# A whole order of steps written anew, with the softmax guards off VectorE and space between steps of VectorE and GpSimd, in an attention and gating kernel

## The chip, the cores and the metric

One core of one Trainium2 chip runs the kernel. The metric is the device time of one execution in microseconds (us). The engines are PE (TensorE matmul; its weight loads are shown apart as PEld), DVE (VectorE), ACT (ScalarE), POOL (GpSimd) and SP (SyncE, which here only issues DMAs). Each works through its own queue in order and waits where an operand or a buffer is not ready.

## What is computed

For each of 8 batches and 8 heads, 512 tokens `x` (64 wide) and 32 states read each other by softmax attention. The joined result, 576 rows of 512 channels, goes through a causal convolution of five taps per channel, a sigmoid gate, a product with `x @ w_val`, and a product with `w_out`.

```python
scores = scale * np.matmul(x, state.transpose(0, 1, 3, 2))
a = np.exp(scores - scores.max(-1, keepdims=True))
a /= a.sum(-1, keepdims=True) + 1e-09
xread = np.matmul(a, state)
...                                   # scores2, a2: the same with x and state exchanged
sread = np.matmul(a2, x)
x = np.concatenate([xread, sread], axis=2)   # then as (8, 576, 512)
gate = 1.0 / (1.0 + np.exp(-gate_pre))       # gate_pre: five taps of conv_w along the sequence
return (gate * (x @ w_val) @ w_out).astype(np.float32)
```

## The kernel before

The work is cut into 882 small steps, 858 of which run. Most of a step is one instruction on ACT, DVE or POOL, or one group of matmuls. A hand-written table of numbers, `ORDER`, gives the one order in which all steps are recorded; every engine's queue is that order with the other engines' steps left out. A letter behind a number picks the engine where the step can run on several: `a` ACT, `v` DVE, `g` POOL. A second table, `PLACES`, gives each tile its buffer: eight PSUM banks `ps0` to `ps7`, and named slots in SBUF. A tile that takes over a slot waits for the last reader of the tile before it. So the two tables set the queues and all the waits; the functions only say what a step does.

For each batch b the steps are: load `xT` and `x`; `scores` (PE, tile `sc`); `scores_T` (DVE transposes it into `sl`), `max_n`, `sub_n`, `exp_n`, `sum_n`, `guard_n` (adds 1e-9 to the sums), `inverse_n`, `scale_n` and `probs` (transposes the probabilities back), which is the softmax over the states; `max_s`, `exp_s`, `sum_s` (the guard of the other softmax, 128x2 numbers), `inverse_s`, and `exp_T`, `state_read`, `state_read_copy`, `state_read_T`, `state_read_out`, which is the states' read. `state_val` (tile `sgv`) multiplies state and `w_val`. `read` (tile `xr`) gives the token's read, from which `gate_first`, `gate_last`, `gate_tap` and `gate_add` make the convolution and `gate` its tanh. `values` (tile `val`) gives the values, `gated` the product, `high` and `low` split it in two parts `gh` and `gl`, `project` (tile `op`) multiplies by `w_out`, and `store` writes 128 rows out. Batch 0 differs: its taps are multiplied into the states beforehand (`tap_state`, tile `z`), and `read_conv` then does read and convolution in 80 matmul records. The weights come as 64-bit words and are made into floats by `words_fold` (ACT), `words_clamp`, `words_low` and `words_join` (DVE). `tail` treats the 256 rows of the states at the end. Eight `warm_up` steps run ahead of the first scores and eight more between the head's matmuls.

The helper functions hold the lines that the profile names: L256, L258 and L260 are `copy` on ACT, DVE and POOL, L264 and L266 `scale`, L269 `combine`, L421, L423 and L425 `guard` on ACT, DVE and POOL. Other lines: L340 warm-up, L386 `scores`, L356 `conv_spread`, L404 `exp_T`, L414 `state_read`, L369 `state_val`, L439 `state_read_T`, L436 `state_read_copy`, L497 `read`, L512 `read_conv`, L537 `gate_tap`, L549 `gate`, L560 `values`, L563 `gated`, L568 to L570 `project`, L449 `scores_T`, L460 `max_n`, L394 `max_s`, L470 `sum_n`, L477 `inverse_n`, L486 and L488 `probs`, L320 and L325 `words_clamp` and `words_join`. This is what uses the tables:

```python
t = PLACE.get(name, tag)                       # in get(): which slot a tile stands in
...
    with tc.manual_schedule(engines=None):
        for step in ORDER:
            engine = ENGINES.get(step[-1])
            fn, args = steps[int(step.rstrip("avg"))]
            fn(*([engine] if engine else []), *args)
...
def guard(e, out, in_):                        # the three forms of a guard
        nc.scalar.activation(out, in_, AF.Identity, bias=ones[:, 1:2])
        nc.vector.tensor_scalar_add(out, in_, EPS)
        nc.gpsimd.tensor_scalar(out, in_, EPS, None, op0=ALU.add)
```

Of the kernel before, what the change touches and what calls it, by code (L numbers as in the profile page):

```python
# [833 lines left out]
```

## Time and profile before

| | |
|---|---|
| time, median of 3 runs | 214.91 us (214.18 to 215.24) |
| the profiled execution | 215.14 us, its span from first to last instruction 213.4 us |
| PE busy | 206.0 us, 97% of the span |
| DVE busy | 175.6 us, 82% |
| POOL busy | 147.8 us, 69% |
| ACT busy | 145.1 us, 68% |
| first matmul of `read_conv` | 19.00 us |
| last matmul | 210.03 us |

Times inside the span count from its first instruction. Busy shares are averages: a busy PE says that matmuls follow each other without idle time, and the waits show where they don't. A row of the timeline gives start, duration, engine, line, instruction, the tile written and the tiles read; in brackets stand the idle time ahead of it and what ended that.

### The profile page before, as it was taken

The page shows a single profiled execution, that of the slowest core. Times are in us where ns is not written, and L with a number is a line of the kernel's source. Part 1 is how long each engine was busy: PE and PEld are TensorE (multiplying, and loading weights), DVE is VectorE, ACT ScalarE, POOL GpSimd, SP SyncE. Part 2 cuts the span into 40 slices and gives each one's busy share as a digit, 9 for nine tenths or more (in the row PEclk, how much of TensorE's full clock was granted, in tenths as well). Part 3 has the DMA queues.
Part 4 walks back from the last instruction along what each step waited for, and adds up shares of the span by engine and source line. Part 5 has one row for each costly group of instructions (what it writes and reads, how often), then busy time and mean ns, then how long its engine had stood idle before and what let it go on. Part 6 is the DMA issues. An engine that isn't in the chain of part 4 may idle for free.

```text
span 213.4 us, 4629 instructions
## 1 busy us (share of the span) xinstructions
PE 206.0 (97%) x1791; PEld 150.2 (70%) x1791; DVE 175.6 (82%) x272; ACT 145.1 (68%) x306; POOL 147.8 (69%) x126
## 2 busy tenths in 40 slices
PE   8977999999999999999999999999999999999994
PEld 8754343876588677877686758688867768898883
DVE  1599898999989898999889999979997997697300
ACT  2298999985995879879947983684666473652511
POOL 1179899879989996879987899784869903620200
PEclk9999999999999999999999999999999999999999
DMA  6989990000346885510009960209400400040326
GB/s 169 397 339 335 410 413 17 0 0 3 107 193 246 292 288 151 206 54 0 3 2 321 382 281 5 98 0 290 155 0 3 151 3 0 0 149 3 146 51 197
DMA packets 9364, 31.25 MB, mean 146 GB/s; under 512 B 1130, under 2 KB 1406, under 8 KB 7422
## 3 DMA queue, kind: packets, MB, share of 16 engines
q1 hardware_dynamic: 9342, 30.96, 40.2%
q8 instruction: 14, 0.23, 0.4%
q14 instruction: 8, 0.07, 0.1%
HBM read 22.04 MB, written 8.91 MB: 145 GB/s over the span
## 4 chain that ended last, share of the span: by engine, by line
PE 86%; DVE 7%; POOL 2%; ACT 2%; issue 1%; DVEq 0%; POOLq 0%; ACTq 0%
PE val L560 19%; PE op L568 13%; PE op L569 13%; PE op L570 13%; PE sgv L369 4%; PE xr L497 3%; PE srp L414 3%; PE sc L386 3%; PE warm L340 3%; PE e2p L404 3%; PE tval L633 3%; PE xr L512 2%; DVE acc L537 2%; DVE r L423 1%; POOL ex L269 1%; ACT acc L532 1%
## 5 line engine op out<-in xcount | busy, mean ns | idle before, releaser
L537 DVE SCALAR_TENSOR_TENSOR acc<-xr,cw,acc 128x511 f32<-128x511 f32 (+2 forms) x84 | 59.8, 737 | 4.4 <-ACT last L264 2.2
L568 PE MATMUL op<-woh,gh 128*128 128x512 f32 (+1 forms) x132 | 52.2, 396 | 0.0
L569 PE MATMUL op<-wol,gh 128*128 128x512 f32 (+1 forms) x132 | 51.2, 388 | 0.0
L570 PE MATMUL op<-woh,gl 128*128 128x512 f32 (+1 forms) x132 | 51.0, 387 | 0.0
L269 POOL TENSOR_TENSOR acc<-acc,last 128x508 f32<-128x508 f32 x24 | 31.2, 1301 | 19.2 <-DVE acc L537 13.7
L269 POOL TENSOR_TENSOR gl<-g,gh 128x512 fp32r<-128x512 f32 x28 | 36.9, 1326 | 8.7 <-ACT gh L256 7.8
L568 PEld LDWEIGHTS op<-woh,gh 128*128 128x128 f32 x132 | 24.9, 189 | 6.3 <-ACT o L256 0.8
L570 PEld LDWEIGHTS op<-woh,gl 128*128 128x128 f32 x132 | 24.8, 188 | 5.5
L569 PEld LDWEIGHTS op<-wol,gh 128*128 128x128 f32 x132 | 24.8, 188 | 4.9
L563 DVE SCALAR_TENSOR_TENSOR g<-sig,val 128x512 f32<-128x512 f32 x32 | 21.6, 682 | 5.0 <-POOL gl L269 2.1
L256 ACT COPY o<-op 128x512 f32<-128x512 f32 (+1 forms) x32 | 18.0, 574 | 9.1 <-PE op L570 7.6
L532 ACT ACTIVATE acc<-xr,cw 128x512 f32<-128x512 f32 x28 | 19.5, 699 | 6.0 <-PE xr L497 4.2
L560 PE MATMUL val<-ah,swh 128*128 128x512 f32 x56 | 23.1, 412 | 0.4 <-ACT last L264 0.4
L549 ACT ACTIVATE sig<-acc 128x512 f32<-128x512 f32 x28 | 17.5, 639 | 7.9 <-POOL acc L269 7.9
L560 PE MATMUL val<-ah,swl 128*128 128x512 f32 x56 | 22.1, 394 | 0.0
L560 PE MATMUL val<-al,swh 128*128 128x512 f32 x56 | 22.0, 393 | 0.0
L264 ACT ACTIVATE last<-xr,cw 128x508 f32<-128x508 f32 x23 | 16.0, 695 | 7.3 <-DVE acc L537 5.5
L269 POOL TENSOR_TENSOR sl<-sl,mx 128x1024 f32<-128x1024 f32 (+1 forms) x8 | 14.5, 1813 | 6.0 <-DVE mx L460 6.0
L269 POOL TENSOR_TENSOR al<-sl,ah 128x1024 fp32r<-128x1024 f32 x7 | 16.8, 2400 | 1.5 <-ACT ah L256 1.4
L256 ACT CAST gh<-g 128x512 fp32r<-128x512 f32 x21 | 12.9, 628 | 6.6 <-DVE g L563 6.5
L269 POOL TENSOR_TENSOR ex<-ex,rc 128x1024 f32<-128x1024 f32 (+1 forms) x9 | 15.5, 1726 | 0.4 <-DVE rc L477 0.4
L560 PEld LDWEIGHTS val<-ah,swh 128*128 128x128 f32 x56 | 10.5, 188 | 5.1 <-issue 2.2
(128 smaller groups left out, 394.4 us busy)
## 6 DMA issues: line engine op xcount, KB each, us to landing
x<-x SPq DMA_DIRECT2D x8, 1024.0 KB, 8.3
out<-o SPq DMA_DIRECT2D x31, 256.0 KB, 2.5
xT<-xT SPq DMA_DIRECT2D x7, 1024.0 KB, 5.6
vw<-w_val SPq DMA_DIRECT2D x4, 512.0 KB, 7.8
ow<-w_out SPq DMA_DIRECT2D x4, 512.0 KB, 7.3
xT<-xT SPq DMA_DIRECT2D x2, 512.0 KB, 5.3
su<-sT SPq DMA_DIRECT2D x2, 256.0 KB, 3.8
z<-z SPq DMA_DIRECT2D x2, 256.0 KB, 7.7
```

The costliest lines, as they stand in the source:

```text
L256: nc.scalar.copy(out, in_)
L264: nc.scalar.mul(out, in_, factor)
L269: (nc.vector if e == "DVE" else nc.gpsimd).tensor_tensor(out, a, b, op=how)
L369: nc.tensor.matmul(get("sgv", b, g)[NS * q:NS * q + NS], su[h, b, q], wv[h, q], start=True, stop=True, tile_position=(D * g, NS * q))
L532: nc.scalar.mul(get("acc", b, pr), pt, cw[:, HALO, pr:pr + 1])
L537: nc.vector.scalar_tensor_tensor(acc[:, d:], get("xr", b, pr)[:, :S - d], cw[:, HALO - d, pr:pr + 1], acc[:, d:], op0=ALU.mult, op1=ALU.add)
L549: nc.scalar.activation(get("sig", b, pr), get("acc", b, pr), AF.Tanh, scale=0.5)
L560: nc.tensor.matmul(get("val", b, k), w, a, start=(i == 0), stop=(i == len(parts) - 1))
L563: nc.vector.scalar_tensor_tensor(get("g", b, k), get("sig", b, k), 1.0, get("val", b, k), op0=ALU.add, op1=ALU.mult)
L568: nc.tensor.matmul(pt, gh, woh[:, k, c], start=(k == 0), stop=False)
L569: nc.tensor.matmul(pt, gh, wol[:, k, c], start=False, stop=False)
L570: nc.tensor.matmul(pt, gl, woh[:, k, c], start=False, stop=(k == NPR - 1))
```

## The change

No function is changed. `ORDER` and `PLACES` are written anew as a whole. Of the 858 steps 77 change their engine: 16 go from ACT to DVE and 12 from ACT to POOL, 12 from DVE to ACT and 13 from DVE to POOL, 12 from POOL to ACT and 12 from POOL to DVE. One warm-up step (860) is added. Among the moved steps are the three guards that ran on DVE, those of batch 6 (`sum_s`) and batch 7 (`sum_s` and `guard_n`), which now run on POOL; no guard is left on DVE. One line shifts: every line number behind the tables is one higher in the changed kernel.

```diff
 ORDER = """
-0 1 2 3 4 5 6 7 8 78 12 11 25 79 40 45 164 35 19 17 14g 21a 20g 81 22 83 26 60 87 91 27a 82 92v 88 84 93 43a 100 28 94
+0 1 2 3 4 5 6 7 8 35 38a 36 11 12 19 21a 20v 22 25 14v 37v 78 79 28 55 40 30 45 164 39 17 81 15a 83 87 91 92g 26 27a
...
 PLACES = """
-al0 vw0_0 vw0_2 al_1 al_3 al_5 al_7
+al0 vw0_2 ow0_0 al_1 al_3 al_5 al_7
...
```

SP issues the loads; these are its first rows before (`vw0_2` is the third block of `w_val`, `ow0_2` of `w_out`, `su` the states, `cww` the taps):

```order
L277 DMA xT_0_110<-xT 128x1024
L285 DMA su_73<-sT 128x512
L300 DMA cww_113<-conv_w 20x128
L277 DMA xT_0_110<-xT 128x1024
L296 DMA vw0_2_117<-w_val 128x512
L296 DMA vw1_3_119<-w_val 128x512
L277 DMA xT_1_121<-xT 128x2048
L296 DMA vw1_1_123<-w_val 128x512
L281 DMA z_72<-z 128x512
```

and after:

```order
L297 DMA vw1_1_110<-w_val 128x512
L301 DMA cww_116<-conv_w 20x128
L286 DMA su_73<-sT 128x512
L278 DMA xT_0_129<-xT 128x1024 x2
L297 DMA ow1_1_134<-w_out 128x512
L297 DMA vw0_2_136<-w_val 128x512
L297 DMA vw0_0_138<-w_val 128x512
L297 DMA vw1_3_140<-w_val 128x512
L278 DMA xT_1_142<-xT 128x2048
L282 DMA z_72<-z 128x512
```

A block of weights now goes ahead of the first half of batch 0's `xT`, and two more blocks ahead of the states `z` that `tap_state` reads.

On POOL in the head, from the first subtraction of batch 0's softmax to `tap_state`, before:

```order
L269 TENSOR_TENSOR sl_0_144<-sl_0_144,mx_0_154 128x2x256
L425 TENSOR_SCALAR sm_0_175<-sm_0_175 128x2x8
L320 TENSOR_SCALAR wc_v_2_181<-wc_v_2_181 128x512
L320 TENSOR_SCALAR wc_v_3_184<-wc_v_3_184 128x512
L269 TENSOR_TENSOR ex_0_168<-ex_0_168,rc_0_191 128x2x256
L425 TENSOR_SCALAR sm_0_175<-sm_0_175 128x2x8
L269 TENSOR_TENSOR ex_0_168<-ex_0_168,rc_0_191 128x2x256
L269 TENSOR_TENSOR z5_0_260<-z_72,cwb_71 128x640
```

and after:

```order
L270 TENSOR_TENSOR sl_0_157<-sl_0_157,mx_0_160 128x2x256
L321 TENSOR_SCALAR wc_o_1_169<-wc_o_1_169 128x512
L270 TENSOR_TENSOR sl_0_157<-sl_0_157,mx_0_160 128x2x256
L426 TENSOR_SCALAR sm_0_195<-sm_0_195 128x2x8
L321 TENSOR_SCALAR wc_v_2_190<-wc_v_2_190 128x512
L270 TENSOR_TENSOR ex_0_188<-ex_0_188,rc_0_242 128x2x256
L321 TENSOR_SCALAR wc_v_0_245<-wc_v_0_245 128x512
L426 TENSOR_SCALAR sm_0_195<-sm_0_195 128x2x8
L321 TENSOR_SCALAR wc_v_3_254<-wc_v_3_254 128x512
L270 TENSOR_TENSOR ex_0_188<-ex_0_188,rc_0_242 128x2x256
L270 TENSOR_TENSOR z5_0_273<-z_72,cwb_71 128x640
```

POOL has both subtractions now, and three clamps of weight blocks between them and `tap_state` in place of two.

On DVE in batch 7, around the guard of its states' softmax, before (`acc_7_3` and `acc_7_0` are convolution sums, `r2_7` the guarded sums):

```order
L537 SCALAR_TENSOR_TENSOR acc_7_3_2199<-xr_7_3_2183,cw_68,acc_7_3_2199 128x510
L423 TENSOR_SCALAR r2_7_2289<-sum2_7_1838 128x2
L537 SCALAR_TENSOR_TENSOR acc_7_3_2199<-xr_7_3_2183,cw_68,acc_7_3_2199 128x509
L537 SCALAR_TENSOR_TENSOR acc_7_0_2221<-xr_7_0_2177,cw_68,acc_7_0_2221 128x509
L431 RECIPROCAL r2_7_2289<-r2_7_2289 128x2
L269 TENSOR_TENSOR gl_6_1_2310<-g_6_1_2169,gh_6_1_2217 128x512
```

and on POOL after, where that guard now stands:

```order
L426 TENSOR_SCALAR sm_7_2000<-sm_7_2000 128x32
L270 TENSOR_TENSOR acc_6_1_1995<-acc_6_1_1995,last_6_1_2054 128x508
L270 TENSOR_TENSOR ex_7_1979<-ex_7_1979,rc_7_2091 128x1024
L426 TENSOR_SCALAR r2_7_2109<-sum2_7_1805 128x2
L261 TENSOR_TENSOR wvh_1163<-wv_65,ones_69 128x512
```

The guard stands there between POOL's `scale_n` of batch 7 and a copy of `w_val`; the split `gl_6_1`, too, is POOL's after the change.

## Rows read from the trace of the kernel before

**Rows 1.** The page: busy time of the engines, with their share of the span.
```profile
PE 206.0 (97%) x1791; PEld 150.2 (70%) x1791; DVE 175.6 (82%) x272; ACT 145.1 (68%) x306; POOL 147.8 (69%) x126
```

**Rows 2.** Waits of PE from 19 us to the end: engine, line, releaser: us in total, times, longest.
```profile
PE xr L512 <- POOL z L269: 1.2, 1, 1.2
PE srT L439 <- ACT sr L436: 0.5, 1, 0.5
PE val L560 <- ACT last L264: 0.4, 1, 0.4
```

**Rows 3.** Busy time by stretch: the stretch, its length, then PE, PEld, DVE, ACT and POOL busy with counts, the granted TensorE clock, the DMA share and GB/s.
```profile
5.33:10.67 5.34, 5.34 (x61) 4.20 (x61) 2.69 (x6) 1.39 (x4) 0.83 (x2) 1.00 1.01 397
16.00:19.00 3.00, 1.78 (x15) 1.41 (x14) 3.00 (x8) 2.96 (x7) 2.64 (x3) 1.00 1.14 348
```

**Rows 4.** Timeline of the head, all engines: warm-up matmuls, the issue of the second half of `xT`, and the first matmuls and softmax steps of batch 0.
```profile
1.03 6.46 PE L340 MATMUL warm<-cwb 128*128 128x128 f32 x32 [1.03 <-DVE cwb L335]
...
2.06 0.35 SPq L277 DMA_DIRECT2D xT<-xT  x1
...
7.43 0.66 PE L386 MATMUL sc<-xT,ss 64*32 64x256 f32 x16
8.02 1.15 PE L356 MATMUL cwbp<-cwf,sel 20*128 20x128 f32 x8
8.18 0.78 DVE L449 STREAM_TRANSPOSE sl<-sc 128x256 f32<-128x256 f32 x2 [1.05 <-PE sc L386]
9.10 0.66 PE L386 MATMUL sc<-xT,ss 64*32 64x256 f32 x16
10.13 2.50 PE L340 MATMUL warm<-ident 128*128 128x128 f32 x20
10.32 0.77 DVE L449 STREAM_TRANSPOSE sl<-sc 128x256 f32<-128x256 f32 x2
11.13 0.69 DVE L460 TENSOR_REDUCE mx<-sl 128x16 f32<-128x512 f32 x1
11.90 1.05 POOL L269 TENSOR_TENSOR sl<-sl,mx 128x512 f32<-128x512 f32 x1 [5.08 <-DVE mx L460]
12.33 1.28 DVE L394 TENSOR_REDUCE nb<-sc 128x1 f32<-128x512 f32 x2
13.04 0.26 POOL L425 TENSOR_SCALAR sm<-sm 128x16 f32<-128x16 f32 x1
13.38 1.19 POOL L320 TENSOR_SCALAR wc_v<-wc_v 128x512 f32<-128x512 f32 x2
14.53 1.05 POOL L269 TENSOR_TENSOR ex<-ex,rc 128x512 f32<-128x512 f32 x1
17.37 1.58 POOL L269 TENSOR_TENSOR z<-z,cwb 128x640 f32<-128x640 f32 x1
```

**Rows 5.** DMA issues of the head, each from a stretch that holds that issue alone: tile, queue, count, KB each, us from issue to landing. First the first half of batch 0's `xT`, then the second half, then the states `z` (issued at 4.93).
```profile
xT<-xT SPq DMA_DIRECT2D x1, 512.0 KB, 4.2
xT<-xT SPq DMA_DIRECT2D x1, 512.0 KB, 6.3
z<-z SPq DMA_DIRECT2D x1, 256.0 KB, 10.5
```

**Rows 6.** Timeline of PE and DVE from `read_conv` to the first `read`.
```profile
19.00 4.54 PE L512 MATMUL xr<-a,z 32*64 32x512 f32 x80 [1.21 <-POOL z L269]
25.48 3.67 PE L560 MATMUL val<-a,sw 128*128 128x512 f32 x8
32.96 0.60 PE L404 MATMUL e2p<-ident,e 128*128 128x128 f32 x4
36.22 1.11 PE L497 MATMUL xr<-sl,z 32*64 32x512 f32 x16
...
29.41 1.23 DVE L486 STREAM_TRANSPOSE sl<-ex 128x1024 f32<-128x1024 f32 x1
```

**Rows 7.** Timeline from 164 to 176 us: POOL, DVE, ACT and PE.
```profile
165.43 2.41 POOL L269 TENSOR_TENSOR al<-sl,ah 128x1024 fp32r<-128x1024 f32 x1
...
165.70 2.17 DVE L423 TENSOR_SCALAR r<-sum 128x2 f32<-128x2 f32 x1
169.16 1.74 DVE L269 TENSOR_TENSOR gl<-g,gh 128x512 fp32r<-128x512 f32 x1
172.41 0.69 DVE L269 TENSOR_TENSOR gl<-g,gh 128x512 fp32r<-128x512 f32 x1
...
168.54 1.34 ACT L264 ACTIVATE last<-xr,cw 128x508 f32<-128x508 f32 x2 [2.40 <-DVE acc L537]
...
169.38 0.27 PE L439 MATMUL srT<-ident,sr 128*128 128x128 f32 x1
170.03 0.47 PE L560 MATMUL val<-ah,swh 128*128 128x512 f32 x1 [0.38 <-ACT last L264]
174.04 0.40 PE L560 MATMUL val<-ah,swl 128*128 128x512 f32 x1
174.90 0.33 PE L439 MATMUL srT<-ident,sr 128*128 128x128 f32 x1 [0.47 <-ACT sr L436]
```

**Rows 8.** Instructions of the guards on POOL (L425): duration in ns, least, median and longest, and when.
```profile
L425 POOL TENSOR_SCALAR r<-sum x4: 218/224/224, 36.9 to 131.2; 128x2 f32<-128x2 f32 x4
```

**Rows 9.** A group of POOL by line and form: the split of `w_out` blocks; busy us, mean ns of one, idle time ahead.
```profile
L269 POOL TENSOR_TENSOR wol<-ws_o,woh 128x512 fp32r<-128x512 f32 x3 | 3.9, 1295 | 0.2
```

More of the change, by code (lines that the diff above doesn't have):

```diff
@@ L102 @@
-last1 last_7_0 last_7_2 tacc_1
-mx0 mx_0 mx_2 mx_4 mx_6
-mx1 mx_1 mx_3 mx_5 mx_7
+al0 vw0_2 ow0_0 al_1 al_3 al_5 al_7
+al1 vw0_0 ow0_2 al_2 al_4 al_6 xtl
+e20 e2_0_0 e2_2_0 e2_4_1 e2_6_0
+e21 e2_0_1 e2_2_1 e2_3_0 e2_4_0 e2_5_0 e2_6_1 e2_7_0
+e22 e2_1_0 e2_1_1 e2_3_1 e2_5_1 e2_7_1
+e2T0 e2T_1_0 e2T_2_0 e2T_3_1 e2T_4_1 e2T_5_1 e2T_6_0 e2T_7_1
+e2T1 e2T_0_1 e2T_2_1 e2T_4_0 e2T_6_1
+e2T2 e2T_0_0 e2T_1_1 e2T_3_0 e2T_5_0 e2T_7_0
+g0 wc_v_1 wc_v_2 wc_v_3 wc_o_3 g_0_0 g_0_1 g_1_2 g_1_3 g_2_1 g_2_2 g_3_1 g_3_2 g_4_0 g_4_1 g_5_1 g_5_3 g_6_0
@@ new lines @@
+g0 g_6_1 g_6_3 g_7_1 tg_1
+g1 wc_conv wc_v_0 wc_o_0 wc_o_1 wc_o_2 g_0_2 g_0_3 g_1_0 g_1_1 g_2_0 g_2_3 g_3_0 g_3_3 g_4_2 g_4_3 g_5_0 g_5_2
+g1 g_6_2 g_7_0 g_7_2 g_7_3 tg_0
+gh0 gh_0_1 gh_1_2 gh_2_1 gh_3_2 gh_4_3 gh_5_1 gh_6_3 gh_7_2
+gh1 gh_0_2 gh_2_3 gh_4_2 gh_6_1 tgh_1
+gh2 gh_0_0 gh_2_2 gh_4_0 gh_6_2 tgh_0
+gh3 gh_0_3 gh_2_0 gh_4_1 gh_6_0
+gh4 gh_1_1 gh_3_0 gh_5_2 gh_7_0
+gh5 gh_1_3 gh_3_1 gh_5_3 gh_7_3
+gh6 gh_1_0 gh_3_3 gh_5_0 gh_7_1
+gl0 gl_0_1 gl_1_2 gl_2_1 gl_3_2 gl_4_3 gl_5_1 gl_6_3 gl_7_2
@@ new lines @@
+gl1 gl_0_2 gl_2_3 gl_4_2 gl_6_1 tgl_1
+gl2 gl_0_0 gl_2_2 gl_4_0 gl_6_0 tgl_0
+gl3 gl_0_3 gl_2_0 gl_4_1 gl_6_2
+gl4 gl_1_1 gl_3_0 gl_5_2 gl_7_0
+gl5 gl_1_3 gl_3_1 gl_5_3 gl_7_3
+gl6 gl_1_0 gl_3_3 gl_5_0 gl_7_1
+last0 last_1_0 last_1_1 last_2_1 last_2_2 last_3_0 last_3_2 last_4_1 last_4_2 last_5_1 last_5_2 last_5_3 last_6_0
+last0 last_7_0 last_7_1 last_7_3 tacc_0
+last1 last_1_2 last_1_3 last_2_0 last_2_3 last_3_1 last_3_3 last_4_0 last_4_3 last_5_0 last_6_1 last_6_2 last_6_3
+last1 last_7_2 tacc_1
@@ L105 @@
+mx0 mx_0 mx_3 mx_5 mx_7
+mx1 mx_1 mx_2 mx_4 mx_6
 nb0 nb_0 nb_4
@@ new lines @@
+ps0 tval_0
+ps1 warm_1 wp_conv cwp halo_0_1 op_0_2 sc_1_1 val_1_1 sc_2_1 e2p_2_0 srp_2 sgv_2_0 op_2_2 e2p_3_0 sgv_3_1 val_3_3
+ps1 srp_4 val_4_1 srp_5 sgv_5_0 val_5_2 op_5_2 op_6_0 e2p_7_0 xr_7_1 op_7_3 warm_17
+ps2 warm_2 cwbp_1 srp_0 xr_0_0 halo_0_2 xr_1_3 val_1_0 val_1_3 op_1_0 op_1_3 srT_2 e2p_3_1 sgv_3_0 val_3_0 op_3_1
+ps2 xr_4_3 e2p_5_0 xr_6_3 sc_7_0 srT_7 xr_7_3 val_7_2 top_1
+ps3 warm_3 sc_0_0 xr_0_2 op_0_3 e2p_1_1 xr_1_1 xr_2_2 sc_3_0 xr_3_3 val_3_2 sc_4_0 sgv_5_1 sc_6_0 sgv_6_0 xr_6_0
@@ new lines @@
+ps3 op_6_3 xr_7_0 op_7_2
+ps4 warm_4 sc_0_1 e2p_0_1 xr_0_3 halo_0_3 srT_1 sc_2_0 sgv_2_1 xr_2_3 val_2_2 val_2_3 srT_3 sc_4_1 e2p_4_1 sgv_4_0
+ps4 xr_4_2 val_4_0 e2p_5_1 srT_5 xr_5_2 op_5_1 e2p_6_1 xr_6_2 sgv_7_1 op_7_0_0
+ps5 warm_5 cwbp_0 wp_v_3 wp_o_2 xr_0_1 xr_1_0 val_2_1 sc_3_1 xr_3_2 val_3_1 e2p_4_0 xr_4_1 op_4_1 op_4_2 xr_5_0
+ps5 val_5_3 val_6_1 op_6_1 e2p_7_1 xr_7_2 top_0 warm_11 warm_13 warm_15 warm_18
+ps6 warm_6 wp_v_0 wp_o_1 wp_o_3 sgv_0_1 val_0_2 srp_1 xr_1_2 xr_2_0 xr_3_1 sgv_4_1 xr_4_0 op_4_3 xr_5_1 val_5_1
@@ L140 @@
 sm1 sm_1 sm_3 sm_5 sm_7
-sum20 sum2_0 sum2_2 sum2_5
-sum21 sum2_1 sum2_7
-sum22 sum2_3
-sum23 sum2_4 sum2_6
+sum20 sum2_0 sum2_6
+sum21 sum2_1 sum2_4
+sum22 sum2_2 sum2_5
+sum23 sum2_3 sum2_7
 swh0 sw0_0 swh_2 swh_4 swh_6
 swh1 swh_1 swh_3 swh_5 swh_7
-swl0 vw1_3 ow1_1 swl_1 swl_3 swl_5 swl_7
-swl1 vw1_1 ow1_3 swl_2 swl_4 swl_6
-x0 x_0 x_3 x_6
-x1 x_1 x_4 wvh
-x2 x_2 x_5 x_7 wvl
-xT0 xT_0 xT_2 xT_4 xT_6
-xT1 xT_1 xT_3 xT_5 xT_7
+swl0 vw1_1 vw1_3 swl_1 swl_3 swl_5 swl_7
+swl1 ow1_1 ow1_3 swl_2 swl_4 swl_6
+x0 x_1 x_3 x_4 x_5 x_6
+x1 x_2 x_7 wvl
+x2 x_0 wvh
+xT0 xT_0 xT_2 xT_7
+xT1 xT_1 xT_3 xT_4 xT_5 xT_6
 """
```

135 lines of the change are left out of this document (48 added, 87 removed).

## The prediction

> **What bounds the kernel now.** I read the page first: PE is busy 97% of the span, DVE 82% [rows 1]. A busy PE need not be at its pace, so next came PE's waits. From 19 us to the end they are three, the first of them the wait that ends at 19.00 and the other two 0.9 us together [rows 2]. So from `read_conv` on PE sets the time, and an engine that gets faster beside it gains nothing. What a new order can still change is of three kinds: how late `read_conv` starts, since in the 3 us ahead of it PE is busy 1.78 us [rows 3] with warm-up and small matmuls; the two late waits; and the end after the last matmul, 3.4 us of copy, store and landing. The last stays: the final half tile is copied by ACT and stored as before (only the first half's copy goes to DVE). The danger is the mirror image: a new wait of PE anywhere after 19 us costs its full length.
>
> The sum is made for the profiled execution, 215.14 us with a span of 213.4; it is 0.23 over the median of the runs shown, 214.91. I work out differences and put them on the median.
>
> **The head, later by 1.3.** Before, the first scores start at 7.43, when the eight warm-up steps end; the first half of `xT`, issued at 0.72, was there 4.2 us later [rows 4, 5]. After, a 512 KB block of `w_val` goes first. The bytes ahead of the first half are then those that stood ahead of the second: that one was issued at 2.06 and took 6.3 us, so 8.4. The scores start 1.0 later, at 8.4. The second half is 512 KB behind it, 1.3 us at 397 GB/s [rows 3], so 9.7; between the two halves PE spreads the taps, 1.08 us from 8.02 to 9.10 [rows 4], so the second scores start at about 10.1. DVE begins their transposes 0.75 later as it did at the first (7.43 to 8.18): 10.85. Before it began them at 10.32, held by a subtraction that now is POOL's, which gives back part of the 1.0.
>
> From there to `tap_state` DVE and POOL hand work to each other. DVE: two transposes 0.77, one `max_s` 0.6 (half of 1.28), `max_n` 0.69, so 12.9. POOL subtracts 1.05 to 13.95. The first sum is ready at 14.2, after another `max_s` and the sum itself on DVE. From then POOL has a row of its own: guard 0.26, clamp 0.6 (half of 1.19), scale 1.05, clamp 0.6, guard 0.26, clamp 0.6, scale 1.05, `tap_state` 1.58, together 6.0 [rows 4]. That ends at 20.2, and with the handoffs `read_conv` starts at 20.3 against 19.00: +1.3. The states `z` have 1 MB more ahead of them: 4.93 + 10.5 = 15.4 before, some 2.6 to 3.1 later now (at 397 and 340 to 348 GB/s) [rows 3, 5], so 18.0 to 18.5, just ahead of `tap_state`'s start at 18.6. From below the term is 0, if the loads come as the first half did, 4.2 us after their issue; from above 2.0, if `z` lands another 0.7 later and holds POOL. I take 1.3: the nearest row is the second half's own 6.3.
>
> **PE's work behind that point, 0.** The instructions are the same but for a warm-up step in the head. Moved past the start of `read_conv` are two `exp_T` (0.44 each to the next step) to behind it, and one `state_val` (1.02) to ahead of it, in time in which PE waits anyway: 0.15 less. Small matmuls stand between large ones in a few more places; a large one that follows a small one takes about 0.1 longer to the next. Between -0.3 and +0.3; 0 is taken.
>
> **The late waits go, -1.2.** At 165.70 DVE's guard of 128x2 numbers takes 2.17 us; POOL's `low` of `al` runs from 165.43 to 167.84, and the guard ends 0.03 later. The same guard takes 0.22 on POOL [rows 7, 8]. `gl_6_1` on DVE then takes 1.74 where another takes 0.69, again beside POOL. ACT waits 2.40 for the taps behind the guard, and PE for ACT: from the transpose at 169.38 to the next matmul 0.65, where hardly 0.1 is needed, and from 174.04 to 174.90 0.86 for 0.23. That is 0.6 and 0.6. The guard and `gl_6_1` both go to POOL. On POOL the guard costs 0.22, behind `scale_n`; from read 7's end to its `state_read_T` PE has 7 us of other work (one `values`, two `project` of 2.8, one `exp_T`) that hide it. If that cover fails, PE waits for ACT's copy as before. The Trainium skill agrees with these rows (SBUF — State Buffer, section Who interferes with whom): the port pair that the two engines share is held for a whole instruction, and the other engine blocks.
>
> **New waits, +0.5.** No row shows them. From below they are 0, as PE had from 19 to 169 us; from above about 2, by what one held DVE instruction cost in rows 7, happening once or twice. The change puts twelve steps from POOL and sixteen from ACT on DVE, among them subtractions and splits of the kind that was held. Their nearest cover is the distance between `probs` and `read`. It was 36.22 - 30.64 = 5.6 us at batch 1 [rows 6]; I take a quarter of the upper bound.
>
> **Sum.** +1.3 + 0 - 1.2 + 0.5 = +0.6: 215.5.
>
> **Rivals.**
> *A wait at the first `read`.* Before, PE had 17.2 us of work from 19.00 to 36.22 [rows 6]. After, only `read_conv` 4.54, three `values` of batch 0 (each half of 3.67) and one `exp_T` 0.5 stand between: 10.5. PE gets there at 30.8. DVE's work to the end of `probs` 1, from 19.5: transposes 1.26, maximum 1.2, the subtraction on DVE now (two of 0.69), three joins 1.9, sum 1.2, one `max_s` 0.6, inverse 0.3, two `gated` 1.2, `probs` 1.2, so 10.2, and some 0.4 of handoffs: 30.1. It decides from a delay of 0.7 on. One POOL split of `w_out` takes 1.30 [rows 9] and stands beside that subtraction. Held once there it costs 0.6, held again at the splits and convolution sums that DVE takes over, 1 to 2. With the head's 1.3 this ends at 216.5 to 217.5: slower, 217.0. For it speaks the short distance, against it that two other joins can move into the hole. By the page named above, a DVE instruction with two inputs in SBUF is blocked by POOL's reads, and this subtraction has two; the page thus speaks for this rival, and no row shows a subtraction on DVE beside a POOL split.
>
> *The head is no later.* If the first half lands while the warm-up still runs (it needs 4.2 us, not 6.3, from an issue near 2.06: 6.3), the second scores begin as before at about 9.1 to 9.5, POOL's row of 6.0 starts nearer 13 than 14.2, and `read_conv` comes at 19.1. Without a new wait that is 214.91 + 0.1 - 1.2 = 213.8. For it speaks that PE waits for `xT` only once in the head; against it that the same bytes took to 8.4.
>
> *The change does not do what it says.* DVE keeps steps that exclude POOL's in the last third, and one of them is held as the guard was: the 1.2 stays, 1.3 + 1.2 - 1.2 + 0.2 gives 216.4.
>
> *The clock falls.* Between the end of the warm-up, near 15.4, and 20.3 PE does two small groups of 1.0 each. The granted clock stood at 1.00, the 2.4 GHz level, in the 3 us with 1.78 us of work [rows 3], so a thinner stretch is untried. The first 32 warm-up matmuls take 0.20 each (6.46 us) and twenty later ones 0.125 (2.50) [rows 4]: at that slower pace `read_conv`'s 4.54 become 7.3, and the time 218.2. The Trainium skill (TensorE: Matmul & The Clock Gate, section What's actually happening) has PE go back to the 1.2 GHz level once it has been idle; it speaks for this rival, and no row shows such a fall.
>
> **How the numbers follow.** My forecast 0.45, the wait at `read` 0.18, a head no later 0.20, the guard's loss staying 0.10, the clock 0.07. The likeliest gives 215.5, by itself 214.9 to 216.2. A measurement of this kernel can tell about 0.5% from no change: 213.84 and 215.98. Of the forecast 0.40 lies within these and 0.05 above; of the head no later 0.12 below and 0.08 within; of the guard's 0.02 within and 0.08 above; the wait and the clock lie above. That makes faster 0.12, same 0.50, slower 0.38. The range goes from 213.7, the head no later, to 217.4, the wait at `read` nearly in full; what is left out is the clock and the outer ends, about 0.2.
>
> **What the profile after would show.** The head: the first scores near 8.4, `tap_state` ending near 20.2, `read_conv` at 20.3; 19.2 or less would make me wrong by 1. The middle: `read` of batch 1 near 30.8 and no PE wait there. The late part: no DVE instruction of a guard, and between 155 and 180 us no PE wait over 0.3. The end: 3.3 to 3.4 us from the last matmul to the span's end. A wait of PE over 1 us after `read_conv`, or a granted clock under 1.00, would make the prediction wrong upward.

## The result and the profile after

The changed kernel takes 217.00 us (median of five executions, 216.23 to 217.84) against 214.46 for the kernel before on the same chip: ratio 1.0108, 95% interval 1.0085 to 1.013. It is 1.1% slower; the time forecast was 215.5. The profiled execution is the longest of the five, 217.84 us with a span of 216.1 us, 2.7 more than before. Where an execution lies over 1.5% above the fastest of its kernel (one each of e3_warm, e4_loads, e5_head and e12_fold_warm below: 220.27, 1140.95, 409.67 and 219.09 us), the ratio leaves it out and the median keeps it; e5_head's is the profiled one and gives no marks.

The page: busy time, and the granted clock in 40 slices of 5.4 us, in tenths (9 is 90% or more). PE is busy for 206.9 us, against 206.0 before [rows 1], and its clock, which was at full level throughout before, dips in the fourth slice.

```profile
PE 206.9 (96%) x1795; PEld 149.9 (69%) x1795; DVE 174.3 (81%) x275; ACT 143.1 (66%) x302; POOL 147.0 (68%) x127
...
PEclk9997999999999999999999999999999999999999
```

Waits of PE over the whole span (us in total, times, longest). All three lie in the head. From `read_conv` on there is none, where before there were two [rows 2]: the late waits are gone and no new one has come.

```profile
PE sc L387 <- DMA xT<-xT: 3.4, 1, 3.4
PE cwbp L357 <- DVE ss L267: 1.3, 1, 1.3
PE warm L341 <- DVE cwb L336: 1.0, 1, 1.0
```

Timeline of PE in the head (start, us, line, operation, idle time before and its releaser), and below it POOL's `tap_state`, which ends at 20.87. The warm-up ends at 15.3, the scores of batch 1 wait 3.39 us for their `xT`, `state_val` takes 2.06 us, and `read_conv` starts at 22.04 (19.00 before, [rows 6]; 20.3 forecast).

```profile
11.02 4.29 PE L341 MATMUL warm<-ident 128*128 128x128 f32 x36
18.69 1.72 PE L387 MATMUL sc<-xT,ss 64*32 64x512 f32 x16 [3.39 <-DMA xT<-xT]
20.05 2.06 PE L370 MATMUL sgv<-wv,su 64*32 64x512 f32 x16
22.04 4.26 PE L513 MATMUL xr<-a,z 32*64 32x512 f32 x72
...
19.32 1.55 POOL L270 TENSOR_TENSOR z<-z,cwb 128x640 f32<-128x640 f32 x1 [0.39 <-DMA z<-z]
```

Busy time by stretch (columns as in [rows 3]). PE does next to nothing from 15 to 19 us, and the granted clock is 0.51 from 19 to 21, its 1.2 GHz level; from 23 on it is back at 1.00.

```profile
15.00:17.00 2.00, 0.30 (x3) 0.11 (x1) 1.69 (x5) 1.54 (x4) 1.92 (x4) 1.00 0.98 377
17.00:19.00 2.00, 0.31 (x8) 0.21 (x16) 1.78 (x5) 2.00 (x6) 1.85 (x3) 1.00 1.05 416
19.00:21.00 2.00, 2.00 (x28) 0.66 (x16) 1.29 (x3) 1.52 (x4) 1.55 (x1) 0.51 1.03 434
21.00:23.00 2.00, 2.00 (x32) 0.48 (x24) 1.97 (x3) 0.99 (x3) 0.61 (x1) 0.64 1.06 377
23.00:25.00 2.00, 2.00 (x48) 0.78 (x40) 1.83 (x3) 2.00 (x4) 0.29 (x1) 1.00 0.95 383
```

Why `xT` is late: the issues on SP, then the first two rows of ACT, and last the kernel before, its table load and its issue of batch 1's `xT`. Three `w_val` loads are issued from 3.41 on, and the third of them stands until 6.8: its buffer is that of the first block, which ACT still reads. ACT in turn was late with it, because its table load of 1.28 us now stands behind the wait for that block (before it ran at 0.71). Batch 1's `xT` (7.21) and `z` (7.70) are queued behind; before they went out at 3.40 and 4.93.

```profile
3.41 3.75 SPq L297 DMA_DIRECT2D vw<-w_val  x3
7.21 0.44 SPq L278 DMA_DIRECT2D xT<-xT  x1
7.70 0.49 SPq L282 DMA_DIRECT2D z<-z  x1
...
4.19 1.28 ACT L314 ACT_TABLE_LOAD   x1 [4.19 <-DMA vw<-w_val]
5.49 0.72 ACT L314 ACTIVATE wp_v<-vw,ones 128x512 int32<-128x512 uint8 x1
...
0.71 1.28 ACT L305 ACT_TABLE_LOAD   x1 [0.71 <-PEq L823]
3.40 0.56 SPq L277 DMA_DIRECT2D xT<-xT  x1
```

The late part, which answers to [rows 7, 8]: first the sum guards on POOL by their line (ns least, median, longest, and when), the last of them at 158.7, clear of the split `al` at 164.88; then PE's timeline, the last transpose of `state_read_T`, 0.23 behind the matmul ahead of it (176.96), and the matmul right behind it, 0.03 us later. Before, 0.65 stood between such a transpose and the next matmul (169.38 to 170.03), and 0.86 between a matmul and the next transpose (174.04 to 174.90).

```profile
L426 POOL TENSOR_SCALAR r<-sum x5: 217/218/225, 26.6 to 158.7; 128x2 f32<-128x2 f32 x5
```

```profile
177.19 0.27 PE L440 MATMUL srT<-ident,sr 128*128 128x128 f32 x1
177.22 0.48 PE L569 MATMUL op<-woh,gh 128*128 128x512 f32 x1
```

The end, first before and then after: SP's last issues and ACT's last copy. Before, the last copy ends at 210.72 and the last store is issued there, at 210.75. After, the copy ends at 213.05, but SP is then at the fifth of five earlier issues that stand back to back from 211.00, and sends the last at 213.37: 0.32 later. From the start of the last matmul to the end of the span it is 3.33 us before (210.03 to 213.36) and 3.73 after (212.32 to 216.05).

```profile
208.58 1.36 SPq L651 DMA_DIRECT2D out<-to  x3
210.04 1.05 SPq L591 DMA_DIRECT2D out<-o  x2
...
210.35 0.37 ACT L256 COPY o<-op 128x256 f32<-128x256 f32 x1 [1.00 <-PE op L570]
```

```profile
211.00 1.81 SPq L652 DMA_DIRECT2D out<-to  x4
212.90 0.87 SPq L592 DMA_DIRECT2D out<-o  x2
...
212.68 0.37 ACT L257 COPY o<-op 128x256 f32<-128x256 f32 x1 [2.27 <-PE op L571]
```

So the span's +2.7 is made of three pieces, read from three marks (start of `read_conv`, start of the last matmul, end): the head +3.04 (19.00 to 22.04), the body between the marks -0.75 (191.03 to 190.28), the end +0.40.

### The profile page after: what moved, and what is told of

It reads as the page before. It is cut to its first block, busy times and chain, and to the rows that moved or that the text cites. A ratio compares the mean times of both kernels' runs of the same rounds, so it can differ in the third digit from the quotient of the medians.

```text
span 216.1 us, 4621 instructions
## 1 busy us (share of the span) xinstructions
PE 206.9 (96%) x1795; PEld 149.9 (69%) x1795; DVE 174.3 (81%) x275; ACT 143.1 (66%) x302; POOL 147.0 (68%) x127
## 3 DMA queue, kind: packets, MB, share of 16 engines
HBM read 22.04 MB, written 8.91 MB: 143 GB/s over the span
## 4 chain that ended last, share of the span: by engine, by line
PE 90%; DMA 7%; ACT 1%; issue 0%; SPq 0%; ACTq 0%
PE val L561 22%; PE op L569 14%; PE op L570 14%; PE op L571 14%; DMA xT<-xT 5%; PE sgv L370 4%; PE srp L415 4%; PE sc L387 4%; PE e2p L405 3%; PE xr L498 3%; PE tval L634 3%; PE xr L513 2%; DMA vw<-w_val 2%; PE top L571 1%; PE top L570 1%; PE top L569 1%
## 5 line engine op out<-in xcount | busy, mean ns | idle before, releaser
L538 DVE SCALAR_TENSOR_TENSOR acc<-xr,cw,acc 128x511 f32<-128x511 f32 (+2 forms) x84 | 61.1, 741 | 6.9 <-ACT last L265 3.6
L270 POOL TENSOR_TENSOR gl<-g,gh 128x512 fp32r<-128x512 f32 x28 | 36.0, 1294 | 15.6 <-ACT gh L257 15.0
L270 POOL TENSOR_TENSOR acc<-acc,last 128x508 f32<-128x508 f32 x25 | 32.0, 1285 | 7.3 <-DVE acc L538 3.7
L561 PE MATMUL val<-ah,swh 128*128 128x512 f32 x56 | 23.7, 424 | 0.0
L270 POOL TENSOR_TENSOR sl<-sl,mx 128x1024 f32<-128x1024 f32 (+1 forms) x8 | 13.6, 1705 | 13.5 <-DVE mx L461 13.5
L257 ACT COPY o<-op 128x512 f32<-128x512 f32 (+1 forms) x29 | 16.6, 583 | 8.3 <-PE op L571 6.7
L561 PE MATMUL val<-ah,swl 128*128 128x512 f32 x56 | 22.1, 394 | 0.0
L265 ACT ACTIVATE last<-xr,cw 128x508 f32<-128x508 f32 x21 | 14.7, 701 | 3.7 <-POOL acc L270 2.5
```

The lines of the kernel that those rows point to most:

```text
L257: nc.scalar.copy(out, in_)
L265: nc.scalar.mul(out, in_, factor)
L270: (nc.vector if e == "DVE" else nc.gpsimd).tensor_tensor(out, a, b, op=how)
L538: nc.vector.scalar_tensor_tensor(acc[:, d:], get("xr", b, pr)[:, :S - d], cw[:, HALO - d, pr:pr + 1], acc[:, d:], op0=ALU.mult, op1=ALU.add)
L561: nc.tensor.matmul(get("val", b, k), w, a, start=(i == 0), stop=(i == len(parts) - 1))
```

## The experiments

Fourteen kernels, each timed beside the kernel before on one chip. A number in the diffs is a step of the order, its letter the engine (v DVE, a ACT, g POOL). The body is the time from the start of `read_conv` to that of the last matmul, the end what follows to the end of the span; these marks come from the one profiled execution of a kernel, which can differ from its median (e2_guards_back: 219.12 against 216.61 us).

| kernel | ratio to before (95%) | `read_conv` | body | end |
|---|---|---|---|---|
| before | 1 | 19.00 | 191.03 | 3.33 |
| changed | 1.0108 (1.0085 to 1.013) | 22.04 | 190.28 | 3.73 |
| e1_guards_off | 0.9959 (0.9946 to 0.9972) | 18.88 | 190.41 | 3.32 |
| e2_guards_back | 1.0101 (1.0066 to 1.0137) | 23.13 | 190.47 | 3.73 |
| e3_warm | 1.0084 (1.0063 to 1.0105) | 20.65 | 190.38 | 3.73 |
| e4_loads | 1.0219 (1.0189 to 1.0249) | 23.26 | 191.84 | 3.70 |
| e5_head | 1.0397 (1.0361 to 1.0434) | | | |
| e6_head_fold | 1.0368 (1.0337 to 1.04) | 19.63 | 197.75 | 3.75 |
| e7_fold | 1.0073 (1.0048 to 1.0099) | 20.35 | 190.13 | 3.73 |
| e8_state_val | 1.0406 (1.037 to 1.0442) | 20.19 | 197.28 | 3.71 |
| e9_head117 | 1.0419 (1.0375 to 1.0463) | 18.89 | 200.60 | 3.79 |
| e10_head256 | 1.0059 (1.0036 to 1.0083) | 18.50 | 191.80 | 3.85 |
| e11_after_head | 1.0152 (1.012 to 1.0185) | 20.90 | 192.84 | 3.33 |
| e12_fold_warm | 1.0077 (1.0051 to 1.0103) | 20.53 | 190.13 | 3.74 |
| e13_end | 1.0085 (1.0055 to 1.0115) | 22.00 | 190.13 | 3.38 |
| e14_all | 1.0069 (1.0043 to 1.0095) | 20.90 | 190.13 | 3.36 |

**The guards alone, in the order before.**

```diff
-638v 723v 729v
+638g 723g 729g
```

> The kernel before, with the guards of sum_s:6, guard_n:7 and sum_s:7 on POOL and not on DVE, nothing else. Theory (the late waits come from DVE's 2.17 us guard beside POOL): about 1 us less, some 213.5 us against 214.5, and the waits of PE near 169 to 170 and 174 us are gone. Rival (the new order of the work took the waits away, not the engine of the guards): no change, 214.3 to 214.7. Second rival (POOL's own queue becomes the wait): 214.7 to 215.5.

Measured 213.95 us against 214.83, ratio 0.9959: 0.9 less. In the profile the body is 0.62 shorter. In POOL's timeline the guard takes 0.22 us just ahead of the split `al`:

```profile
165.44 0.22 POOL L425 TENSOR_SCALAR r<-sum 128x2 f32<-128x2 f32 x1
165.74 2.41 POOL L269 TENSOR_TENSOR al<-sl,ah 128x1024 fp32r<-128x1024 f32 x1
```

Of PE's two late waits one is left:

```profile
PE srT L439 <- ACT sr L436: 0.4, 1, 0.4
```

The one that ended near 170, behind the 2.17 us guard of [rows 7], is gone. The other, near 174, is not, so half of the theory fell; `gl_6_1` stays on DVE here and takes 1.50 us. Ahead of that wait stands ACT, which waited 0.71 us for an addition on DVE (1.42 us here, 0.68 before). What ends this wait in the changed order, the engine of `gl_6_1` or the order, was not tried. This kernel is faster than both kernels of the study.

**The same guards back on DVE, in the changed order.**

```diff
-638g 723g 729g
+638v 723v 729v
```

> The changed kernel with the same three guards back on DVE, its order kept. Theory (the engine of the guards): 0.5 to 1.2 us more than the changed kernel's 217.0, so 217.5 to 218.2, with waits of PE after 160 us. Rival (the order alone gives the room): 216.8 to 217.2 and no late wait.

Measured 216.61 us, ratio 1.0101, as the changed kernel; no PE wait over 0.3 us after 25 us, body 190.47 against 190.28. (`read_conv` at 23.13 is that of an execution whose granted clock stood at 0.50 to 0.69 from 11 to 17 us.) The two sum guards on DVE by their line:

```profile
L424 DVE TENSOR_SCALAR r<-sum x2: 158/536/914, 138.1 to 156.8; 128x2 f32<-128x2 f32 x2
```

One of them still takes 0.91 us, but PE waits for neither. So the engine of the guards is worth 0.9 us in the order before and nothing in the changed one: there the order alone gives the room, as the rival has it.

**Warm-up matmuls in the idle time.**

```diff
-859 860 166
+859 860 861 862 863 864 865 866 867 166
```

> The changed kernel with seven more warm-up steps (28 matmuls, 0.477 us a step by the 4.29 us of the 36 that are there) between the warm-up and the scores of batch 1, so that PE works while it waits for the transfer. Theory (part of the head's 3.0 us is the lower granted clock that follows PE's idle 3.4 us): the granted clock stays 1.0, the scores still start near 18.7, state_val takes 1.0 and not 2.06 us, read_conv starts 0.8 to 1.3 us earlier, 215.7 to 216.2 us. Rival (the late transfers alone make the head late): 216.8 to 217.2.

Measured 216.65 us, ratio 1.0084. PE's timeline, and then the stretch from 19 us:

```profile
10.94 7.41 PE L342 MATMUL warm<-ident 128*128 128x128 f32 x64
18.41 1.09 PE L388 MATMUL sc<-xT,ss 64*32 64x512 f32 x16
19.29 1.34 PE L371 MATMUL sgv<-wv,su 64*32 64x512 f32 x16
```

```profile
19.00:21.00 2.00, 1.98 (x40) 0.53 (x27) 2.00 (x5) 2.00 (x6) 1.59 (x1) 1.00 0.99 367
```

With PE at work up to the scores, the clock stays at 1.00, the scores take 1.09 and not 1.72, `state_val` 1.34 and not 2.06, and `read_conv` starts 1.39 earlier in the profiled execution, as the theory had it. The time did not follow as far: 216.65 lies between the theory's range and the rival's, and the ratios differ by 0.24% only (0.5 us), with intervals that overlap. Why the gain of the profiled execution does not show in full in the times is not settled. The changed kernel itself kept its clock in one execution of five (216.23 us, mean granted clock 0.999; the other four, at 0.992, took 216.97 to 217.84).

**The late loads first.**

```diff
-30 45 164 39 17
+30 164 17 45 39
```

> The changed kernel with the loads of batch 1's xT and of z issued ahead of the fourth w_val load, which waits for a buffer that ACT gives back near 6.8 us. Theory (this queue order makes the head late): xT of batch 1 lands near 15.9 and z near 16.5 us (18.55 and 19.19 in the changed kernel), PE is idle for less than 1 us after the warm-up, the granted clock stays 1.0, and read_conv starts at 19 to 20.3 us (the fourth block lands near 17.7 and state_val waits for it): 214.0 to 215.3 us. Rival (the chain of exponentials, guards and the join on ACT, DVE and POOL holds the head): read_conv at 21.5 us or later, 216.5 us or more.

Measured 219.7 us, ratio 1.0219: worse, and the theory fell as it stood. `xT` of batch 1 comes 2.1 us earlier, but the fourth `w_val` block now comes last. PE's waits:

```profile
PE sgv L370 <- DVE wv L326: 3.1, 1, 3.1
PE sc L387 <- DMA xT<-xT: 1.2, 1, 1.2
```

`state_val`, which stands ahead of `read_conv` on PE in this order, needs all four blocks. The wait has moved from `xT` to `wv`, and behind it the clock falls all the same (0.50 from 21 to 25 us). So moving these loads alone does not help as long as `state_val` comes first; other orders of the loads were not tried.

**`state_val` and the fourth block behind `read_conv`.** Three kernels: with the loads moved too, with these and the first block folded before it is shifted, and with the loads as they are.

```diff
-98 46 65 32g 104g 33a 105 47g 48a 29a
+98 65 32g 104g 33a 105 29a
-86 49 122g 108 107 90 119 72a 167 170 173 51 52g 123 120a
+86 122g 108 107 90 123 46 47g 48a 167 170 173 49 119 72a 51 52g 120a
```

> The changed kernel with the loads of batch 1's xT and of z ahead of the fourth w_val load, and with that block's fold, clamp, shift and join and with state_val:0 behind read_conv:0 on their engines (read_conv and the scores_T of batch 1 don't wait for that block any more). Theory (two things made the head late together: the queue order of the loads, and that the weights of state_val stand ahead of read_conv): scores of batch 1 at 16.6, read_conv at 19.3 to 19.9 us, no wait of 3 us, ratio to the kernel before 0.995 to 1.002, 213.6 to 215.0 us. Rival (the loads are simply too many bytes ahead of batch 1's work, and the wait turns up behind read_conv, at the first values or gated weights): 216 us or more.

> As the kernel with both head edits, and with the first w_val block folded before it is shifted on ACT, so that ACT's table load (1.28 us at 4.19, behind the wait for that block) can run at the start. Theory (the table load delays the chain of conv weights, first scores and exponentials by 1.2 us): first scores near 7.4 (8.59), read_conv at 18.2 to 18.8 us, 0.8 to 1.2 us less than with the head edits alone. Rival (z and xT of batch 1 set the head, not the chain): the same time as with the head edits alone, within 0.3 us.

> The changed kernel with its loads as they are, and with the fourth w_val block's fold, clamp, shift and join and state_val:0 behind read_conv:0. Theory (z, landing at 19.2 and turned into tap_state by 20.9, and xT of batch 1 at 18.6 are the rest of the delay): read_conv starts at 20.9 to 21.1 instead of 22.04 us, 215.6 to 216.3 us. Rival (the transfers alone make the head late, state_val's place is worth nothing): 216.8 to 217.2 us. Second rival (state_val's place is the whole): read_conv at 19 to 20 us, 214.0 to 215.2 us.

Measured 223.55, 222.7 and 223.89 us: the worst of the study but for one. `read_conv` does start earlier (20.19 in e8_state_val, 19.63 in e6_head_fold), but PE then waits at the first values. PE's and ACT's timelines of e8_state_val:

```profile
20.19 6.50 PE L513 MATMUL xr<-a,z 32*64 32x512 f32 x80 [0.19 <-POOL z L270]
26.62 1.09 PE L370 MATMUL sgv<-wv,su 64*32 64x512 f32 x16
29.99 5.40 PE L561 MATMUL val<-a,sw 128*128 128x512 f32 x8 [2.27 <-DVE ws_o L326]
...
27.80 0.60 ACT L265 ACTIVATE sw<-sgv 128x512 f32<-128x512 f32 x1 [7.47 <-PE sgv L370]
28.43 0.71 ACT L314 ACTIVATE wp_o<-ow,ones 128x512 int32<-128x512 uint8 x1
```

ACT takes its steps in their order: the copy of `state_val`'s result stands ahead of the shift of a `w_out` block, so ACT is idle for 7.47 us, and that block's PSUM bank is the one in which the values are due. `read_conv` takes 6.50 us, with a granted clock of 0.50 to 0.69 from 19 to 25 us. These kernels change more than one thing: they show that the wait turns up elsewhere, not what `state_val`'s place alone is worth.

**The table load out of the way.**

```diff
-35 38a 36 11
+35 36 38a 11
```

> The changed kernel with nothing but the first w_val block folded before it is shifted on ACT. Theory (the transfer of batch 1's xT holds the head of the changed kernel, the table load costs nothing there): the first scores start 1.2 us earlier, near 7.4, scores of batch 1 still near 18.5, 216.6 to 217.3 us. Rival (the chain behind the table load holds the head, or the buffer that ACT gives back earlier lets the loads go earlier): 215.6 to 216.0 us.

Measured 216.31 us, ratio 1.0073: between theory and rival. ACT's and PE's timelines:

```profile
0.72 1.28 ACT L306 ACT_TABLE_LOAD   x1 [0.72 <-PEq L824]
4.05 0.67 ACT L306 ACTIVATE wc_v<-vw 128x512 f32<-128x512 f32 x1 [2.05 <-DMA vw<-w_val]
...
17.41 1.09 PE L387 MATMUL sc<-xT,ss 64*32 64x512 f32 x16 [2.27 <-DMA xT<-xT]
```

The first scores start at 8.42 (8.59 in the changed kernel), not at 7.4: their own `xT` holds them, and for them the table load cost 0.17 at most. But the buffer comes free earlier, batch 1's `xT` is issued near 6.0 and its scores start at 17.41 (18.69).

**Both small cures.**

```diff
-35 38a 36 11
+35 36 38a 11
-859 860 166
+859 860 861 862 863 864 865 166
```

> The changed kernel with both small cures of its head: the first w_val block folded before it is shifted on ACT (so that the table load runs at the start), and five more warm-up steps (2.4 us) before the scores of batch 1. Theory (what the two brought one by one, ratios 1.0073 and 1.0084 against 1.0108, has the same cause in part, the granted clock after PE's idle time): ratio 1.004 to 1.0065, 215.4 to 215.9 us, granted clock 1.0 throughout, read_conv near 20.3 us. Rival (the two are one and the same): 1.007 to 1.0085, 216.0 to 216.3 us.

Measured 216.37 us, ratio 1.0077: the rival, they don't add. The clock did not stay up throughout either: in four of the eleven executions its mean was 0.984 to 0.992. In the profiled one `xT` of batch 1 no longer holds the head. POOL's and PE's timelines:

```profile
17.31 0.61 POOL L321 TENSOR_SCALAR wc_v<-wc_v 128x512 f32<-128x512 f32 x1
17.89 1.05 POOL L270 TENSOR_TENSOR ex<-ex,rc 128x512 f32<-128x512 f32 x1
18.90 1.58 POOL L270 TENSOR_TENSOR z<-z,cwb 128x640 f32<-128x640 f32 x1
...
20.53 3.68 PE L513 MATMUL xr<-a,z 32*64 32x512 f32 x64 [0.60 <-POOL z L270]
```

POOL works almost without a gap to `tap_state`'s end at 20.5, and PE waits for that. Before, `tap_state` started at 17.37 [rows 4]: two clamps of `w_val` blocks stood ahead of it there, three here. This is the head as the forecast had it (`tap_state` to 20.2, `read_conv` at 20.3).

**Heads and bodies exchanged.** The first 117 steps of the order before with the rest of the changed one; the same with 256; and the first 141 steps of the changed order with the rest of the one before. Buffers are shifted where two tiles would meet.

```diff
-ORDER = the changed order
+ORDER = the first n steps of one order, then the steps that are left in the order of the other
```

> The first 117 steps of the order before (loads, conversions, the softmax of batch 0, warm-up, scores of batch 1, read_conv:0, state_val:0), then all steps that are left in the changed order; the buffers are shifted where two of its tiles would meet. Theory (the head is the whole of the loss; the changed order behind it is worth its late waits, 1.2 us, less 0.4 at the end): read_conv at 19.0 us, no wait of PE after 160 us, ratio to the kernel before 0.993 to 0.998, 213.0 to 214.1 us. Rival (the changed body only fits its own head; waits turn up where the two orders meet, between 25 and 45 us): 215 to 217 us.

> The same with the first 256 steps of the order before (to the scores_T of batch 3), so that the two orders meet in the middle of batch 1's gate and not in the loads. Theory: as with 117 steps, read_conv at 19.0 us and ratio 0.993 to 0.998, 213.0 to 214.1 us, without waits in the head. Rival (what the changed order gains lies in its first 256 steps too, the meeting place costs): 214.5 us or more.

> The mirror: the first 141 steps of the changed order (its loads, conversions, batch 0 up to the first gated values), then all steps that are left in the order before, with its guards on DVE. Theory (the head alone costs 3.0 us): read_conv at 21.5 to 22.1 us, the waits of PE near 169 and 174 us (by then 3 us later) are back, ratio 1.011 to 1.016, 217.0 to 218.0 us. Rival (the slack of the order before takes up a late head): 215.0 to 216.0 us.

With 117 steps 224.23 us, ratio 1.0419: `read_conv` starts at 18.89, and then the first values wait 6.71 us for `state_val`'s copy, which ACT comes to behind the `w_out` blocks. It is the rival, and tells nothing of the body.

With 256 steps 215.9 us, ratio 1.0059: no late wait, `read_conv` even 0.50 earlier than before, and yet slower than before. Its body takes 191.80, 1.67 more than the 190.13 of the changed order in its own place (e7_fold). From `read_conv` to 55.8 us PE's starts are those of the kernel before, 0.50 earlier; from 74 us on they follow the changed order's to within 0.2. In between, where the two orders meet, a `read` takes 1.92 us (1.21 before), and values wait for a copy on ACT:

```profile
55.87 1.92 PE L497 MATMUL xr<-sl,z 32*64 32x512 f32 x16
71.99 0.50 PE L560 MATMUL val<-ah,swh 128*128 128x512 f32 x1 [0.35 <-ACT o L256]
```

The theory that the changed order behind the old head gives 213.0 to 214.1 fell with this kernel, as the rival has it. What the changed body would win behind the old head without such a meeting place, it doesn't tell.

The mirror, the changed head with the body before, takes 218.5 us, ratio 1.0152, as the theory has it (the time itself 0.5 above), and the two late waits are back, 0.5 and 0.4 us. But `read_conv` starts at 20.90, earlier than the 21.5 to 22.1 expected, and the body is 1.81 longer than before:

```profile
20.90 5.09 PE L512 MATMUL xr<-a,z 32*64 32x512 f32 x80
38.00 2.23 PE L369 MATMUL sgv<-wv,su 64*32 64x512 f32 x16
```

Of the span's 3.71, 1.90 lie ahead of `read_conv`, 0.55 in it (the clock is at 0.50 from 19 to 21 us and at 0.72 to 23), and some 1.1 from 36 us on, where the two orders meet and a `state_val` takes 2.23 us instead of 1.09. So the whole loss lies in the first 41 us, but no more than 2.45 of the 3.71 are the head's own.

**The two stores.**

```diff
-846 850a 789 851 847a 700 803 790v
+846 700 803 850a 789 851 847a 790v
```

> The changed kernel with two stores of the output (store:6,0 and store:7,3) moved ahead of the two copies and stores of the tail's result, where the order before has them or their like. Theory (the last five store issues of the changed kernel, 0.42 to 0.47 us each on SP, stand back to back from 211.0 us, so that the very last goes out 0.3 us after its copy is done): the last half store is issued as soon as its copy ends, 0.3 us less after the last matmul, ratio 1.0085 to 1.0100 against the changed kernel's 1.0108. Rival (the end of the program waits for the bytes on their way, not for the issue): no change, 1.0100 to 1.0115.

Measured 216.85 us, ratio 1.0085; the interval holds the changed kernel's ratio, but the profile is clear. SP's and ACT's last rows:

```profile
212.06 1.17 SPq L592 DMA_DIRECT2D out<-o  x2
...
212.48 0.37 ACT L257 COPY o<-op 128x256 f32<-128x256 f32 x1 [2.27 <-PE op L571]
```

The last store goes out at 212.88, 0.03 after the copy (0.32 in the changed kernel), and the end is 3.38 us: the 0.4 of the end is the queue of store issues.

**Everything that helped.**

```diff
-35 38a 36 11
+35 36 38a 11
-859 860 166
+859 860 861 862 863 864 865 166
-846 850a 789 851 847a 700 803 790v
+846 700 803 850a 789 851 847a 790v
```

> The changed kernel with everything that helped or should help: the first w_val block folded before it is shifted, five more warm-up steps, and the two stores earlier. Theory (what is left of the loss is POOL's row in the head, three clamps of w_val blocks, the second scale of the exponentials and tap_state, which end near 20.4 us, against the 0.7 us that the body wins): read_conv at 20.3 to 20.6 us, ratio 1.0045 to 1.0070. Rival (the parts don't add): 1.0070 to 1.0085.

Measured 216.26 us, ratio 1.0069, at the theory's upper end. Its profiled execution has `read_conv` at 20.90, 0.3 later than expected, since the scores still wait:

```profile
18.64 1.09 PE L387 MATMUL sc<-xT,ss 64*32 64x512 f32 x16 [1.28 <-DMA xT<-xT]
```

The body is 190.13 and the end 3.36: against before +1.90 - 0.90 + 0.03 = +1.03, which is the span's 214.4 against 213.4. Its twelve executions also bear on the clock: seven with a mean granted clock of 0.997 or more took 215.33 to 216.35 us (mean 215.7), five at 0.992 took 216.70 to 217.23 (mean 217.0), 1.3 us more. Told apart in the same way, the changed kernel (four against one) gives 1.0 and e12_fold_warm 1.4, but e2_guards_back and e7_fold only 0.1. Where in the program the clock fell is seen in the profiled executions alone.

## Why the prediction was wrong

**What failed is the head's term**: +1.3 forecast, +3.04 in the profile. The working followed the softmax of batch 0 over DVE and POOL to `tap_state`, and `z`, and put `read_conv` behind that. It never followed PE's own row: `scores` of batch 1 and `state_val` stand ahead of `read_conv` on PE (the text put `state_val` "in time in which PE waits anyway"), and the first of them waits for an `xT` that is queued on SP behind a load that waits for ACT. The chain that was worked out was right in itself: where PE is kept from the other wait, `read_conv` starts at 20.35, 20.53 and 20.65 (e7_fold, e12_fold_warm, e3_warm) against the 20.3 forecast. What comes on top in the profiled execution is late data and the clock: `z` ends its transfer at 19.19, not at 18.0 to 18.5, so `tap_state` ends at 20.87, which is about the upper bound of 2.0 that the text gave for the term; the rest to 22.04, 1.2 us, is PE still at `scores` and `state_val` at half its clock. The profiled execution of e14_all shows this last part apart: its scores start as late, at 18.64, but with the clock at 1.00, and `read_conv` starts at 20.90.

**The rival of the clock** was in the text, with 0.07 and at 218.2. It came true in the profiled execution and, by the mean granted clock of 0.992, in three more of the five, in a smaller size: the working slowed the whole of `read_conv` (4.54 to 7.3), while the run had the lower level over the scores, `state_val` and the start of `read_conv` only. That is 1.2 us ahead of `read_conv` and 0.15 in it (body 190.28 against 190.13 in e7_fold, whose clock stayed up), close to the 1.3 of e14_all. The condition that the text gave for it, two small groups in 5 us, became thinner still by the wait that the text had missed. The Trainium skill (TensorE: Matmul & The Clock Gate, section What's actually happening) says that an idle PE goes back to 1.2 GHz; the traces agree, with 0.51 of the clock granted after 3.39 idle us.

**PE's work behind `read_conv`, 0, and the late waits, -1.2**: right in kind, a little less in size. Summed by kind of step from `read_conv` on, each from its start to the next one's, e7_fold against before, `state_read_T` and the values give -0.89, the moved `exp_T`, `state_val` and scores -0.20 (-0.15 forecast), the other steps +0.19: body -0.90. The cause of the first of the two waits is shown: alone in the old order the guards' new engine takes it away (e1_guards_off, body -0.62), and their old engine costs nothing in the new order (e2_guards_back), so either keeps the guard from holding up PE. The second wait stays in e1_guards_off; it is gone in the changed kernel, but the text's account of it is not shown. The sentence from the Trainium skill on the port pair that DVE and POOL share (SBUF — State Buffer, section Who interferes with whom) agrees with the first: 2.17 us on DVE beside POOL's split of 2.41 [rows 7], 0.22 on POOL ahead of the split.

**New waits, +0.5**: none came; PE waits for nothing from `read_conv` to the end. The rival of a wait at the first `read` fell with it: `read` of batch 1 starts at 32.45 with no wait, 10.4 behind `read_conv` (10.5 forecast). That the measured 217.00 is the very time of this rival (217.0), and lies in the stated range up to 217.4, is chance: none of it comes from that wait. The rival that the head is no later fell, and so did the one that the guard's loss stays.

**The end** was said to stay at 3.3 to 3.4 us, since the last copy and store are as before. It is 3.73: two other stores had been moved in between (e13_end). It was not looked at in SP's queue, though the order showed it.

So in numbers, forecast against found in the profiled execution: head 1.3 and 3.04, late waits and PE's work -1.2 and -0.75 (-0.9 at full clock), new waits 0.5 and 0, end 0 and 0.40; sum 0.6 and 2.7. The median's 2.5 us (217.00 less 214.46) is a little less.

**What stays open.** What `state_val`'s place ahead of `read_conv` costs by itself is not settled, since every attempt to move it made a new wait behind it (e5_head, e6_head_fold, e8_state_val). Nor is it settled why extra warm-up matmuls keep the clock in some executions of a kernel and not in others, or why a lower mean clock costs 1.3 us in some kernels and 0.1 in others. That the changed head is the loss rests on the marks of the profile and on the cures of its parts (e3_warm, e7_fold, e12_fold_warm), which take back up to 0.35% of the 1.1%; the two exchanges (e10_head256, e11_after_head) lose time where the orders meet and don't settle it.

## What to carry to other kernels

A step's start is the latest of all the rows that lead to it: beside the chain of the data, follow the waiting engine's own queue back instruction by instruction, each with its transfer, and each transfer with what holds its issue. A load that waits for a buffer stops every load behind it in its queue, and an idle TensorE can pay a second time through its clock. Of a large reordering, try the small part that has a measured cause by itself: here three letters brought 0.4% and the whole new order lost 1.1%.

## What the runs showed of the hardware

- ACT's table load (1.28 us) runs at 0.72 us when the first activation of the program folds a block, and at 4.19, behind the wait for the transfer, when the first one shifts it (e7_fold against the changed kernel). The order of two activations with the same input decided it.
- In the changed kernel the granted clock was 0.51 from 19 to 21 us, after 3.39 us without a matmul, 0.64 from 21 to 23 and 1.00 from then on, with PE at work all the while. In the profiled execution of e7_fold, 2.27 idle us in the same place left it at 1.00, while in e11_after_head it fell to 0.50 after 2.42, and in e2_guards_back to 0.61 from 9 to 11 us and 0.50 behind that, after waits of 0.82 and 0.90 us.
- The last store issues on SP in the changed kernel took 0.37 to 0.43 us each and started 0.44 to 0.52 us apart, so that five of them delayed the sixth by 0.32 us; with two of them moved ahead the delay is 0.03 (e13_end).
